# Expert weights prepared beside a dense block: steps queued behind the h copies, splits one step later, maxima in other banks

## The chip, the cores and the metric

The kernel runs on one core of a Trainium2 chip. The metric is the device time of one execution in microseconds (us); the time before is 1370.19 us, the median of 3 runs (1365.73 to 1371.75). The engines are PE (matmul), DVE (vector), ACT (scalar), POOL and SP, which issues most of the transfers.

## What is computed

Three layers follow one another. B = 8, H = 8, S = 576, D = 64; the 4608 tokens of 512 features that leave the first go through a dense layer of 2048 features and then through one of 8 experts of 1024 features each.

```python
kv = np.einsum('bhsd,bhse->bhde', k, v)
out = np.einsum('bhsd,bhde->bhse', q, kv)
rms = np.sqrt(np.mean(out * out, axis=-1, keepdims=True) + 1e-06)
x = (out / rms * g_norm).transpose(0, 2, 1, 3).reshape(B * S, H * D)
h = x @ w_in
g = np.maximum(h, 0.0) + alpha * np.minimum(h, 0.0)
x = g @ w_out
logits = x @ w_gate
e_idx = np.argmax(logits, axis=1)
...
for e in range(E):
    mask = e_idx == e
    h = np.maximum(x[mask] @ w1[e], 0.0)
    out[mask] = gate_w[mask, None] * eom[mask, e, None] * (h @ w2[e])
```

## The kernel before

Every large product is made in halves: each operand is split into a high and a low part in 16 bits, each scaled by a power of two taken from the operand's maximum, and three products (high by high, high by low, low by high) are summed.

The tokens are worked in 12 blocks of 384, three tiles of 128. Blocks 0 and 1 follow a plan written by hand, in which w_in and w_out are loaded and split (up to about 210 us). For each of the blocks 2 to 10 an h block is emitted and then a y block, and a scheduler that simulates the engines chooses the order on each engine within what the dependences and the buffers allow. Block 11's products stand in the order of the code. After it, from about 950 us, come the experts' own products, which read the prepared weights `ws` back from memory ("lanes").

An **h block** has 16 pieces. A piece is 12 products of 128x384 (line 688) into one of the two banks of `ps_h`; ACT copies the bank out as `m` (line 693), DVE bends it to `r` (line 702), ACT writes the high half of `g` (line 707) and DVE the low half (line 708). The pool `tp` holds two `m` and two `r`. The bank comes free with `m`. A **y block** has three tiles of 48 products of 128x512 (line 723) in the two banks of `ps_y`; ACT copies a tile out as `ysb` (line 735), and `y_tail` scales it to 16 bits (`row`, lines 775 and 779) and has SP transpose it (`yT`, line 788). The logits `l` (line 801) of a tile need yT and use the one bank of `ps_l`; DVE reads them out as `lg` (line 802), and `rk` (line 835) are counts for routing.

Beside these, `tick` hands out other work, one step at a time, after each piece of h and after every fifth f of a y tile. One kind is the **attention** of a later block: `kvps` (line 262, products of k and v), its maximum `allmaxkv` (lines 150 to 158), `kv` in 16 bits, then for each tile `ops` (line 349, products of kv with the transposed `qT`), `xs` (lines 358 and 399), `x` in halves (lines 410 and 415) and its transpose on SP (line 421), which is what the next h block multiplies. `x_3` is block 3's. qT is transposed on SP too (line 333).

The other kind is `expert_jobs`, the **expert weights**: 16 weight halves m (w1 and w2 of 8 experts), each in four parts of 128x1024. A step is either a magnitude (a raw load `rawe`, line 612, 512 KB, issued by SP; ACT takes absolute values, `eab`, line 623; DVE folds them into a running maximum `eam`, line 626) or a split (ACT `whi`, line 474; DVE `wlo`, line 475; two stores to `ws`, line 642, from ACT and SP). Between a weight's four magnitudes and its four splits stands its maximum: a transpose on PE (line 150, `allmax_w`), a reduction on DVE (`amrow`, line 152) and a product that spreads the result (line 154), in the bank `ps_l`. `tick(f % 3 == 0)` hands out an expert step after every third piece of h, `tick(1)` one after every fifth f of a y tile: 6 and 9 a block. Five raw parts fit in the pool `rawp`; the first magnitude of a weight issues the load of a part that is needed eight steps later in the list, and its first three splits each one that is needed five steps later.

Of the kernel before, what the change touches and what calls it, by code (L numbers as in the profile page):

```python
# [66 lines left out]
def body(ctx: ExitStack, tc, q, k, v, g_norm, w_in, w_out, alpha, w_gate, w_og, w1, w2, out):  # L67
# [79 lines left out]
    def all_max(am, nm):  # L147
        n = am.shape[1]
        ps = ps_l.tile([P, P + E], F32, tag="l", name="allmax" + nm)
# [327 lines left out]
    def finish_max(am, nm):  # L477
        m = small.tile([P, 1], F32, tag="amx", name="amx" + nm)
        dve.tensor_reduce(out=m, in_=am, axis=AX.X, op=ALU.max)
        return all_max(m, nm)  # L480
# [122 lines left out]
    def expert_jobs():  # L603
# [12 lines left out]
        for n in range(4):  # L616
            load(n)
        for m in range(2 * E):
            nm = f"_w{m}"
            am = cv.tile([P, 512], BF16, tag="acc", name="eam" + nm, bufs=1)  # L620
            for i in range(4):
                ab = cv.tile([P, 2, 512], BF16, tag="c", name=f"eab{nm}_{i}", bufs=3)
                act.activation(out=ab.rearrange("p a b -> p (a b)"), in_=raws[4 * m + i], func=AF.Abs)  # L623
                for h in range(2):
                    if i or h:
                        dve.tensor_tensor(out=am, in0=am if i else ab[:, 0, :], in1=ab[:, h, :], op=ALU.max)
                if i == 0:
                    load(4 * m + 4)
                yield
            for w in (256,):  # L630
                dve.tensor_tensor(out=am[:, 0:w], in0=am[:, 0:w], in1=am[:, w:2 * w], op=ALU.max)
            r = finish_max(am[:, 0:256], nm)
            s = small.tile([P, 1], F32, tag="es", name="es" + nm)
            inv = small.tile([P, 1], F32, tag=f"ei{m % 2}", name="ei" + nm)
            pow2(r, nm, s, inv)
            for i in range(4):
                w = ws[m // 2, :, m % 2 * 8192:(m % 2 + 1) * 8192].rearrange("p (t c) -> p t c", t=2)
                hi = stg.tile([P, 1024], F16, tag="hl", name=f"whi{nm}_{i}")
                lo = cv.tile([P, 1024], F16, tag="am", name=f"wlo{nm}_{i}")
                split(hi, lo, raws[4 * m + i], s)  # L640
                for t, (eng, x) in enumerate(((act, hi), (sp, lo))):
                    eng.dma_start(out=w[:, t, i * 1024:(i + 1) * 1024], in_=x)
                if i < 3:
                    load(4 * m + 5 + i)
                yield
            if m % 2 == 0:
                inv1 = inv
            else:
                dve.scalar_tensor_tensor(out=kexp[:, m // 2:m // 2 + 1], in0=inv1, scalar=1.0 / CB, in1=inv,
                                         op0=ALU.mult, op1=ALU.mult)  # L650


    attq, yq, exq, side = [], [], [], []

# [10 lines left out]
    def tick(n_expert=0):  # L665
        if yq:
            yq.pop(0)()
        if side:
            side.pop(0)()
        step(attq)  # L670
        for _ in range(n_expert):
            step(exq)
# [26 lines left out]
    def h_bend(f, part):  # L699
        i, r0 = part  # L700
        r = tp.tile([P, BLK], F32, tag="r", name=f"r_{i}_{f}")
        dve.scalar_tensor_tensor(out=r, in0=r0, scalar=alphat[:, f:f + 1], in1=r0, op0=ALU.mult, op1=ALU.max)  # L702
# [7 lines left out]
    def emit_h_block(i):  # L710
        for f in range(NF):
# [13 lines left out]
    def emit_y_block(i):  # L725
        b = y_state(i)
        for u in range(TB):
# [766 lines left out]
```

## Time and profile before

| what | value |
|---|---|
| runs, median (lowest, highest) | 1370.19 us (1365.73, 1371.75) |
| the profiled execution's own time | 1362.63 us |
| its span | 1360.9 us |
| PE busy | 1266.7 us, 93% |
| DVE busy | 827.1 us, 61% |
| ACT busy | 558.3 us, 41% |
| POOL busy | 333.1 us, 24% |
| bytes moved | 236.22 MB |

The profile follows one execution, and its time stands in the table beside the runs; the span is from its first to its last instruction. Busy shares are means over the whole span, so a stage has to be read from its own windows. A wait is the idle time of an engine just ahead of an instruction, put down to whatever released it last.

### The profile page before, as it was taken

How to read it: one execution, taken by the hardware profiler on the slowest of the kernel's cores; microseconds unless marked ns; L12 is line 12 of the kernel's file. 1: busy time of each engine (PE TensorE's matmuls, PEld its weight loads, DVE VectorE, ACT ScalarE, POOL GpSimd, SP SyncE). 2: the span in 40 equal slices, each digit the busy share in tenths (PEclk: the TensorE clock that was granted, in tenths of full speed). 3: DMA queues.
4: the chain of work that ended last, by engine and by line, in shares of the span. 5: the costliest groups of instructions: out<-in, count | busy, mean ns of one | idle time of the engine just before them, and what ended most of it. 6: DMA issues, size and time to landing. Idle time of an engine off the chain costs nothing. (4 is left out here: it accounts for less than half of the span.)

```text
span 1360.9 us, 21940 instructions
## 1 busy us (share of the span) xinstructions
PE 1266.7 (93%) x7681; PEld 660.8 (49%) x7681; DVE 827.1 (61%) x2316; ACT 558.3 (41%) x928; POOL 333.1 (24%) x410
## 2 busy tenths in 40 slices
PE   5588999949999998999999999999989999999998
PEld 4444455525555554555555555554434444444443
DVE  7999876768787887968687778562612221211221
ACT  3455663436454655655464656450111111111111
POOL 4312220332222232223132222102322222222211
PEclk9799999979999999999999999999989999999999
DMA  9653217647495956775736665306999799699852
GB/s 290 168 162 118 70 63 182 136 143 183 149 245 136 250 162 192 194 225 140 236 66 181 171 179 147 110 9 189 221 339 235 149 289 289 145 237 221 158 108 55
DMA packets 322497, 236.22 MB, mean 174 GB/s; under 512 B 245436, under 2 KB 278220, under 8 KB 317904
## 3 DMA queue, kind: packets, MB, share of 16 engines
q1 hardware_dynamic: 303760, 189.05, 55.5%
q0 software_dynamic: 9216, 28.94, 6.7%
q10 hardware_dynamic: 9408, 16.79, 3.7%
q8 instruction: 62, 1.02, 0.3%
q14 instruction: 51, 0.42, 0.1%
HBM read 248.34 MB, written 53.25 MB: 222 GB/s over the span
## 5 line engine op out<-in xcount | busy, mean ns | idle before, releaser
L723 PE MATMUL y<-wo,g 128*128 128x512 f16 x1728 | 401.2, 380 | 9.7 <-DVE xs L399 7.4
L688 PE MATMUL h<-x,wi 128*128 128x384 f16 x1920 | 340.3, 328 | 24.0 <-DMA x<-x 18.3
L688 PEld LDWEIGHTS <-wi 128*128 128x128 f16 x2304 | 221.7, 98 | 182.7 <-issue 35.7
L723 PEld LDWEIGHTS <-g 128*128 128x128 f16 x1728 | 164.8, 98 | 194.0 <-issue 9.9
L1200 DVE CAST h_d<-br_d 128x512 f16<-128x512 f32 x62 | 27.1, 438 | 259.8 <-ACT br_d L1198 132.7
L1216 PE MATMUL bo_d<-lane,hT_d 128*128 128x512 f16 x744 | 167.3, 382 | 7.5 <-DMA hT_d<-h_d 7.5
L1194 PE MATMUL bh_d<-lane,byT_d 128*128 128x512 f16 x744 | 165.3, 379 | 0.0
L707 ACT CAST g<-r 128x384 f16<-128x384 f32 x192 | 97.3, 509 | 131.4 <-DVE r L702 127.0
L702 DVE SCALAR_TENSOR_TENSOR r<-m,alphat 128x384 f32<-128x384 f32 x192 | 122.2, 639 | 20.5 <-ACT m L693 19.8
L1216 PEld LDWEIGHTS <-hT_d 128*128 128x128 f16 x744 | 72.8, 98 | 97.8 <-DMA hT_d<-h_d 9.0
L1194 PEld LDWEIGHTS <-byT_d 128*128 128x128 f16 x744 | 72.7, 98 | 88.1 <-issue 0.8
L375 POOL TENSOR_TENSOR rs<-ms,mhalf 128x8 f32<-128x8 f32 x36 | 66.4, 1848 | 185.5 <-DVE qm L381 138.0
L693 ACT ACTIVATE m<-h,scal 128x384 f32<-128x384 f32 x160 | 91.9, 575 | 36.0 <-PE h L688 34.0
L708 DVE TENSOR_TENSOR g<-r,g 128x384 f16<-128x384 f32 x160 | 91.7, 575 | 22.6 <-ACT g L707 21.6
L475 DVE SCALAR_TENSOR_TENSOR wlo_w<-rawe,es_w,whi_w 128x1024 f16<-128x1024 f32 x64 | 84.6, 1338 | 19.9 <-ACT whi_w L474 9.8
L867 POOL DMA_INDIRECT ytab<-row,pos x36 | 38.2, 1061 | 216.1 <-DVE pos L848 113.2
L1198 ACT ACTIVATE br_d<-bh_d 128x512 f32<-128x512 f32 x62 | 37.0, 597 | 131.0 <-PE bh_d L1194 109.2
L623 ACT ACTIVATE eab_w<-rawe 128x1024 bf16<-128x1024 f32 x64 | 67.1, 1055 | 47.3 <-DMA rawe<-in_moe_w_dram 45.3
L474 ACT ACTIVATE whi_w<-rawe,es_w 128x1024 f16<-128x1024 f32 x64 | 70.9, 1142 | 29.3 <-DVE es_w L144 15.7
L1220 POOL DMA_INDIRECT out_dram<-ob_d,oidx_d x31 | 31.4, 1013 | 206.2 <-ACT ob_d L1219 189.6
L1219 ACT ACTIVATE ob_d<-bo_d,msc_d 128x512 f32<-128x512 f32 x31 | 21.3, 687 | 139.9 <-PE bo_d L1216 139.9
L688 PE MATMUL hbank<-x,wi 128*128 128x384 f16 x384 | 67.0, 332 | 7.2 <-DMA x<-x 5.4
(365 smaller groups left out, 1367.9 us busy)
## 6 DMA issues: line engine op xcount, KB each, us to landing
lane<-ws SPq DMA_DIRECT2D x150, 1024.0 KB
rawe<-in_moe_w_dram SPq DMA_DIRECT2D x64, 512.0 KB
ws<-whi_w ACTq DMA_DIRECT2D x64, 256.0 KB
ws<-wlo_w SPq DMA_DIRECT2D x64, 256.0 KB
rawwi<-in_moe_w_in_dram SPq DMA_DIRECT2D x16, 512.0 KB
rawwo<-in_moe_w_out_dram SPq DMA_DIRECT2D x16, 512.0 KB
q<-in_q_dram SPq DMA_DIRECT2D x16, 512.0 KB
k<-in_k_dram SPq DMA_DIRECT2D x28, 256.0 KB
```

The costliest lines, as they stand in the source:

```text
L375: pool.tensor_tensor(out=rs, in0=ms, in1=mhalf, op=ALU.pow)
L474: act.activation(out=dst_h, in_=src, func=AF.Copy, scale=s)
L475: dve.scalar_tensor_tensor(out=dst_l, in0=src, scalar=s, in1=dst_h, op0=ALU.mult, op1=ALU.subtract)
L623: act.activation(out=ab.rearrange("p a b -> p (a b)"), in_=raws[4 * m + i], func=AF.Abs)
L688: pe.matmul(ps, wi[:, f // 4 * NC + c, w, fs], xt[i][:, xc, :], start=(n == 0), stop=(n == 3 * NC - 1))
L693: act.activation(out=r0, in_=ps, func=AF.Copy, scale=(scst if start else scal)[:, f:f + 1])
L702: dve.scalar_tensor_tensor(out=r, in0=r0, scalar=alphat[:, f:f + 1], in1=r0, op0=ALU.mult, op1=ALU.max)
L707: act.copy(out=hi, in_=r)
L708: (pool if start else dve).tensor_tensor(out=lo, in0=r, in1=hi, op=ALU.subtract)
L723: pe.matmul(ps, g[:, t, f % GF, us], wo[:, f, w, :], start=(start and m == 0), stop=(stop and m == 2), **kw)
L1194: pe.matmul(hp[ts], j["yT"][:, x, ts], w1_[:, w, c, hs], start=(m == 0), stop=(m == 3 * NC - 1))
L1216: pe.matmul(po[ts], hT[:, g, ts], w2_[:, w, f, :], start=(m == 0), stop=(m == 3 * NFE - 1))
```

## The change

Three things change. Each expert step's instructions on ACT and DVE are ordered behind the last h copy (or y copy) on ACT and the last bend on DVE that had been emitted when the step was handed out. The steps are listed in another order: magnitude 0 of the next weight stands ahead of the four splits of a weight, the maximum is taken in the step of the fourth magnitude, and each of the four splits issues one load, of the part that is five further on and needed four steps later; five parts are loaded at the start instead of four. And a weight's maximum takes its bank from `ps_y` while an h block is emitted and from `ps_h` while a y block is emitted, instead of from `ps_l`.

```diff
-    def all_max(am, nm):
+    def all_max(am, nm, pool_=None, tag="l"):
         n = am.shape[1]
-        ps = ps_l.tile([P, P + E], F32, tag="l", name="allmax" + nm)
+        ps = (pool_ or ps_l).tile([P, P + E], F32, tag=tag, name="allmax" + nm)
...
     def expert_jobs():
...
-        for n in range(4):
-            load(n)
-        for m in range(2 * E):
-            nm = f"_w{m}"
-            am = cv.tile([P, 512], BF16, tag="acc", name="eam" + nm, bufs=1)
-            for i in range(4):
-                ab = cv.tile([P, 2, 512], BF16, tag="c", name=f"eab{nm}_{i}", bufs=3)
-                act.activation(out=ab.rearrange("p a b -> p (a b)"), in_=raws[4 * m + i], func=AF.Abs)
-                for h in range(2):
-                    if i or h:
-                        dve.tensor_tensor(out=am, in0=am if i else ab[:, 0, :], in1=ab[:, h, :], op=ALU.max)
-                if i == 0:
-                    load(4 * m + 4)
-                yield
-            for w in (256,):
-                dve.tensor_tensor(out=am[:, 0:w], in0=am[:, 0:w], in1=am[:, w:2 * w], op=ALU.max)
-            r = finish_max(am[:, 0:256], nm)
...
+        def scale(m):
+            nm = f"_w{m}"
+            am = sums.pop(m)
+            dve.tensor_tensor(out=am[:, 0:256], in0=am[:, 0:256], in1=am[:, 256:512], op=ALU.max)
+            r = finish_max(am[:, 0:256], nm, *idle[0])
...
+        def halves(m, i):
+            nm = f"_w{m}"
+            w = ws[m // 2, :, m % 2 * 8192:(m % 2 + 1) * 8192].rearrange("p (t c) -> p t c", t=2)
+            hi = stg.tile([P, 1024], F16, tag="hl", name=f"whi{nm}_{i}")
+            lo = cv.tile([P, 1024], F16, tag="am", name=f"wlo{nm}_{i}")
+            split(hi, lo, raws[4 * m + i], scs[m][0])
+            for t, (eng, x) in enumerate(((act, hi), (sp, lo))):
+                eng.dma_start(out=w[:, t, i * 1024:(i + 1) * 1024], in_=x)
+            load(4 * m + 5 + i)
+
+        for n in range(5):
+            load(n)
+        magnitude(0, 0)
+        yield
+        for m in range(2 * E):
+            for i in range(1, 4):
+                magnitude(m, i)
+                if i == 3:
+                    scale(m)
+                yield
+            if m + 1 < 2 * E:
+                magnitude(m + 1, 0)
+                yield
             for i in range(4):
...
-                if i < 3:
-                    load(4 * m + 5 + i)
+                halves(m, i)
                 yield
...
+    paced, idle = {}, [None]
...
-        for _ in range(n_expert):
-            step(exq)
+        if n_expert and exq:
+            with ExitStack() as behind_h:
+                for ins in paced.values():
+                    behind_h.enter_context(tc.issue_after(ins))
+                step(exq)
...
-        act.activation(out=r0, in_=ps, func=AF.Copy, scale=(scst if start else scal)[:, f:f + 1])
+        t = act.activation(out=r0, in_=ps, func=AF.Copy, scale=(scst if start else scal)[:, f:f + 1])
+        paced["act"] = t.ins
...
+        paced["dve"] = t.ins
...
     def emit_h_block(i):
+        idle[0] = ps_y, "y"
...
     def emit_y_block(i):
         b = y_state(i)
+        idle[0] = ps_h, "h"
...
-                act.copy(out=ysb, in_=ps)
+                paced["act"] = act.copy(out=ysb, in_=ps).ins
```

Lines of the changed kernel are 21 to 25 higher from `h_sum` on (the h product is line 709, m 714, g 730, the y product 747, ysb 760, l 826), and eab is line 624.

On ACT, in block 5, the magnitudes of weight 6 stand like this before (`m_5_5` is the copy of piece 5 of block 5, `eab_w6_1` the magnitude of part 1 of weight 6, `g` the high half):

```order
L693 ACTIVATE m_5_5_5510<-h_5_5_5497,scal_145 128x384
L623 ACTIVATE eab_w6_1_5701<-rawe_25_5264 128x1024
L707 CAST g1_200<-r_5_4_5460 128x384
L693 ACTIVATE m_5_6_5539<-h_5_6_5526,scal_145 128x384
L707 CAST g1_200<-r_5_5_5512 128x384
L358 ACTIVATE xs_2_2_5477<-ops_2_2_5464 128x512
L623 ACTIVATE eab_w6_2_5797<-rawe_26_5342 128x1024
L288 CAST kv16_5_5396<-kvsc_5_5394 128x512
L707 CAST g1_200<-r_5_6_5541 128x384
L693 ACTIVATE m_5_7_5564<-h_5_7_5551,scal_145 128x384
L623 ACTIVATE eab_w6_3_5840<-rawe_27_5443 128x1024
```

and like this now:

```order
L714 ACTIVATE m_5_12_5676<-h_5_12_5663,scal_145 128x384
L624 ACTIVATE eab_w6_1_5701<-rawe_25_5339 128x1024
L730 CAST g3_202<-r_5_12_5678 128x384
L714 ACTIVATE m_5_13_5718<-h_5_13_5705,scal_145 128x384
L730 CAST g3_202<-r_5_13_5720 128x384
L714 ACTIVATE m_5_14_5737<-h_5_14_5724,scal_145 128x384
L730 CAST g3_202<-r_5_14_5739 128x384
L714 ACTIVATE m_5_15_5791<-h_5_15_5778,scal_145 128x384
L624 ACTIVATE eab_w6_2_5797<-rawe_26_5440 128x1024
L624 ACTIVATE eab_w6_3_5840<-rawe_27_5548 128x1024
L624 ACTIVATE eab_w7_0_5874<-rawe_28_5613 128x1024
```

The magnitude `eab_w6_1` stood behind piece 5 and two more were between pieces 6 and 8; now it stands behind piece 12, and the next three behind piece 15.

On PE, in block 3, y products of the same block (`y_3_0`, `y_3_1`) stand between the pieces of h before, runs of one name left out:

```order
L688 MATMUL h_3_5_3591<-x_3_2516,wi_203 128x384
...
L723 MATMUL y_3_0_3910<-wo_204,g0_199 128x512
...
L801 MATMUL l_2_0_3381<-wg16_147,yT_2_0_3171 128x32
...
L688 MATMUL h_3_6_3620<-x_3_2516,wi_203 128x384
...
L723 MATMUL y_3_1_4048<-wo_204,g0_199 128x512
...
L723 MATMUL y_3_0_3910<-wo_204,g1_200 128x512
...
L723 MATMUL y_3_1_4048<-wo_204,g1_200 128x512
...
L688 MATMUL h_3_7_3643<-x_3_2516,wi_203 128x384
```

and none do now, where only the logits of block 2 come between:

```order
L709 MATMUL h_3_4_3539<-x_3_2516,wi_203 128x384
...
L709 MATMUL h_3_5_3591<-x_3_2516,wi_203 128x384
...
L826 MATMUL l_2_2_3742<-wg16_147,yT_2_2_3412 128x32
...
L709 MATMUL h_3_6_3620<-x_3_2516,wi_203 128x384
...
L709 MATMUL h_3_7_3643<-x_3_2516,wi_203 128x384
```

The y products that stood between pieces 5 and 7 have moved behind the h block, as `y_3_0` now takes its bank after the maximum of a weight.

On PE, from the end of block 5 to the second product of attention in block 6, the first row of each name as it comes (the products of `ops_2_3`, `ops_2_4` and `ops_2_5` are those of three tiles of attention) is this before:

```order
L349 MATMUL ops_2_3_6001<-kv16_4_4440,qT_2_3_5836 128x128
...
L723 MATMUL y_5_1_5938<-wo_204,g3_202 128x512
...
L723 MATMUL y_5_2_6062<-wo_204,g0_199 128x512
...
L688 MATMUL h_6_0_6167<-x_6_5121,wi_203 128x384
...
L349 MATMUL ops_2_4_6186<-kv16_5_5396,qT_2_4_5910 128x128
...
L801 MATMUL l_5_0_6135<-wg16_147,yT_5_0_5936 128x32
...
L688 MATMUL h_6_1_6241<-x_6_5121,wi_203 128x384
...
L688 MATMUL h_6_2_6260<-x_6_5121,wi_203 128x384
...
L150 MATMUL allmax_w7_6222<-ident_62,amx_w7_6220 1x128
...
L349 MATMUL ops_2_5_6325<-kv16_5_5396,qT_2_5_6092 128x128
...
L688 MATMUL h_6_3_6279<-x_6_5121,wi_203 128x384
```

and this now:

```order
L349 MATMUL ops_2_3_5999<-kv16_4_4437,qT_2_3_5836 128x128
...
L747 MATMUL y_5_0_5803<-wo_204,g3_202 128x512
...
L150 MATMUL allmax_w6_5847<-ident_62,amx_w6_5845 1x128
...
L747 MATMUL y_5_1_5934<-wo_204,g3_202 128x512
...
L747 MATMUL y_5_2_6062<-wo_204,g0_199 128x512
...
L826 MATMUL l_5_0_6135<-wg16_147,yT_5_0_5932 128x32
...
L349 MATMUL ops_2_4_6201<-kv16_5_5393,qT_2_4_5906 128x128
...
L826 MATMUL l_5_1_6374<-wg16_147,yT_5_1_6060 128x32
...
L150 MATMUL allmax_w7_6152<-ident_62,amx_w7_6150 1x128
...
L709 MATMUL h_6_0_6182<-x_6_5121,wi_203 128x384
...
L349 MATMUL ops_2_5_6322<-kv16_5_5393,qT_2_5_6092 128x128
```

Between `ops_2_3` and `ops_2_5` there stood y_5_2 and three pieces of h, split by logits; now y_5_2, two sets of logits and one piece of h stand there, and the maxima of weights 6 and 7 are both taken in this stretch.

## Rows read from the trace of the kernel before

**Rows 1.** Page, part 1: busy us of each engine, share of the span, instructions.

```profile
PE 1266.7 (93%) x7681; PEld 660.8 (49%) x7681; DVE 827.1 (61%) x2316; ACT 558.3 (41%) x928; POOL 333.1 (24%) x410
```

**Rows 2.** Windows: busy us (instructions) of each engine, granted clock; two h stretches, a y stretch.

```profile
384.60:436.90 52.30, 49.22 (x356) 27.94 (x355) 45.68 (x135) 29.80 (x51) 12.66 (x9) 1.00 0.73 189
356.40:384.60 28.20, 25.67 (x154) 12.46 (x155) 19.50 (x46) 12.87 (x17) 6.78 (x9) 1.00 0.82 211
872.00:917.10 45.10, 45.10 (x284) 25.49 (x283) 25.82 (x77) 20.06 (x38) 3.23 (x8) 1.00 0.13 31
305.00:950.00 645.00, 625.38 (x4012) 338.81 (x4012) 483.83 (x1409) 340.75 (x553) 154.90 (x144) 0.99 0.61 167
```

**Rows 3.** Windows of line 723 alone, the y products, in h stretches 2 and 4.

```profile
210.70:261.70 51.00, 10.32 (x43) 4.31 (x44) 1.00 0.68 166
384.60:436.90 52.30, 13.31 (x52) 4.84 (x52) 1.00 0.73 189
```

**Rows 4.** Waits of PE, 305 to 950 us: us in total, times, longest.

```profile
PE h L688 <- ACT m L693: 5.6, 7, 2.0
PE ops L349 <- DMA qT<-q: 5.3, 4, 2.5
PE l L801 <- DMA yT<-row: 5.1, 4, 2.3
PE allmax_w L150 <- DVE lg L802: 2.3, 2, 1.4
PE y L723 <- DVE g L708: 0.9, 1, 0.9
```

**Rows 5.** Waits of PE, 210.7 to 305.1 us.

```profile
PE kvps L262 <- DMA v<-in_v_dram: 0.9, 2, 0.5
```

**Rows 6.** Line 623, the magnitudes on ACT: idle before them (us, times), one releaser.

```profile
  DMA rawe<-in_moe_w_dram: 45.3, 30
```

**Rows 7.** Timeline of ACT: start, us, operation, idle before it and its releaser.

```profile
417.62 1.06 ACT L623 ACTIVATE eab_w<-rawe 128x1024 bf16<-128x1024 f32 x1 [1.87 <-DMA rawe<-in_moe_w_dram]
```

**Rows 8.** Timeline of PE at four places.

```profile
242.62 0.23 PE L349 MATMUL ops<-kv,qT 128*128 128x128 f16 x1 [0.20 <-DMA qT<-q]
...
284.20 0.38 PE L158 MATMUL allmaxkv<-amdiagkv,ones 8*128 8x8 f32 x2
...
305.02 6.12 PE L688 MATMUL h<-x,wi 128*128 128x384 f16 x23 [17.36 <-DMA x<-x]
...
419.68 2.11 PE L688 MATMUL h<-x,wi 128*128 128x384 f16 x12 [2.01 <-ACT m L693]
...
520.68 0.83 PE L349 MATMUL ops<-kv,qT 128*128 128x128 f16 x12
521.36 11.20 PE L723 MATMUL y<-wo,g 128*128 128x512 f16 x51
...
543.39 0.73 PE L349 MATMUL ops<-kv,qT 128*128 128x128 f16 x10 [0.55 <-DMA qT<-q]
```

**Rows 9.** Timeline of SP's queue at two places.

```profile
300.47 2.00 SPq L421 DMA_TRANSPOSE x<-x  x1
...
540.18 1.26 SPq L333 DMA_TRANSPOSE qT<-q  x1
```

**Rows 10.** Lines of DVE, 305 to 950 us: busy us, mean ns, idle before.

```profile
L702 DVE SCALAR_TENSOR_TENSOR r<-m,alphat 128x384 f32<-128x384 f32 x144 | 90.8, 631 | 12.9 <-ACT m L693 12.6
L708 DVE TENSOR_TENSOR g<-r,g 128x384 f16<-128x384 f32 x144 | 82.9, 577 | 18.9 <-ACT g L707 18.1
...
L475 DVE SCALAR_TENSOR_TENSOR wlo_w<-rawe,es_w,whi_w 128x1024 f16<-128x1024 f32 x60 | 78.6, 1327 | 19.1 <-ACT whi_w L474 9.5 <-ACT row L775 3.7 <-DMA ws<-wlo_w 3.0
...
L626 DVE TENSOR_TENSOR eam_w<-eam_w,eab_w 128x512 bf16<-128x512 bf16 x86 | 36.8, 428 | 19.1 <-ACT eab_w L623 18.7
```

**Rows 11.** Windows at two waits of PE: PEclk is the granted clock.

```profile
420.00:422.00 2.00, 2.00 (x14) 1.17 (x12) 2.00 (x8) 1.13 (x3) 0.00 (x0) 1.00 0.22 68
767.00:770.00 3.00, 3.00 (x24) 1.99 (x25) 1.94 (x8) 0.45 (x1) 0.00 (x0) 0.50 1.01 249
```

More of the change, by code (lines that the diff above doesn't have):

```diff
@@ L475, in split, with finish_max @@
         dve.scalar_tensor_tensor(out=dst_l, in0=src, scalar=s, in1=dst_h, op0=ALU.mult, op1=ALU.subtract)
-    def finish_max(am, nm):
+    def finish_max(am, nm, *bank):
         m = small.tile([P, 1], F32, tag="amx", name="amx" + nm)
         dve.tensor_reduce(out=m, in_=am, axis=AX.X, op=ALU.max)
-        return all_max(m, nm)
+        return all_max(m, nm, *bank)
     class Dense:
@@ L614, in load, with magnitude @@
                 raws[n] = t
-        for n in range(4):
-            load(n)
-        for m in range(2 * E):
+        sums, scs = {}, {}
+        def magnitude(m, i):
             nm = f"_w{m}"
-            am = cv.tile([P, 512], BF16, tag="acc", name="eam" + nm, bufs=1)
-            for i in range(4):
-                ab = cv.tile([P, 2, 512], BF16, tag="c", name=f"eab{nm}_{i}", bufs=3)
-                act.activation(out=ab.rearrange("p a b -> p (a b)"), in_=raws[4 * m + i], func=AF.Abs)
-                for h in range(2):
-                    if i or h:
-                        dve.tensor_tensor(out=am, in0=am if i else ab[:, 0, :], in1=ab[:, h, :], op=ALU.max)
-                if i == 0:
-                    load(4 * m + 4)
-                yield
-            for w in (256,):
-                dve.tensor_tensor(out=am[:, 0:w], in0=am[:, 0:w], in1=am[:, w:2 * w], op=ALU.max)
-            r = finish_max(am[:, 0:256], nm)
+            if i == 0:
+                sums[m] = cv.tile([P, 512], BF16, tag="acc", name="eam" + nm, bufs=1)
+            am = sums[m]
+            ab = cv.tile([P, 2, 512], BF16, tag="c", name=f"eab{nm}_{i}", bufs=3)
+            act.activation(out=ab.rearrange("p a b -> p (a b)"), in_=raws[4 * m + i], func=AF.Abs)
+            for h in range(2):
+                if i or h:
+                    dve.tensor_tensor(out=am, in0=am if i else ab[:, 0, :], in1=ab[:, h, :], op=ALU.max)
+        def scale(m):
[3 more added lines that the diff above has]
+            r = finish_max(am[:, 0:256], nm, *idle[0])
             s = small.tile([P, 1], F32, tag="es", name="es" + nm)
@@ L635, in expert_jobs @@
             pow2(r, nm, s, inv)
-            for i in range(4):
[L637 to L642, printed above, removed]
-                if i < 3:
-                    load(4 * m + 5 + i)
-                yield
[L646 to L650, printed above, removed]
+            scs[m] = s, inv
+            if m % 2:
+                dve.scalar_tensor_tensor(out=kexp[:, m // 2:m // 2 + 1], in0=scs[m - 1][1], scalar=1.0 / CB, in1=inv,
+                                         op0=ALU.mult, op1=ALU.mult)
+        def halves(m, i):
[20 more added lines that the diff above has]
+                yield
+            for i in range(4):
+                halves(m, i)
+                yield
     attq, yq, exq, side = [], [], [], []
+    paced, idle = {}, [None]
     def step(gens):
@@ L701, in h_bend @@
         r = tp.tile([P, BLK], F32, tag="r", name=f"r_{i}_{f}")
-        dve.scalar_tensor_tensor(out=r, in0=r0, scalar=alphat[:, f:f + 1], in1=r0, op0=ALU.mult, op1=ALU.max)
+        t = dve.scalar_tensor_tensor(out=r, in0=r0, scalar=alphat[:, f:f + 1], in1=r0, op0=ALU.mult, op1=ALU.max)
+        paced["dve"] = t.ins
         return r
```

## Prediction

> **What bounds the kernel now.** I read the engines' busy time first: PE works 1266.7 us of the 1360.9 us span, DVE 827.1 [rows 1]. The change touches only the stretch in which expert weights are prepared beside the h and y blocks, 160 to 870 us. From 305 to 950 us PE is busy 625.4 of 645 us, so not 20 us of waits are there to be won, 17.4 of which are one wait at its start. Next I split that stretch: in the h stretch of block 4 PE has 49.2 of 52.3 us and DVE 45.7, in the y stretch ahead of it PE 25.7 of 28.2 and DVE 19.5 [rows 2]. DVE is nearly as full as PE in an h stretch and far from it in a y stretch. It doesn't bind there today because y products, 52 matmuls and 13.3 us of PE in block 4, 43 and 10.3 us in block 2, stand between the pieces of h [rows 3].
>
> Third, the waits of PE: for the copy m out of the h bank 5.6 us in 7 waits, for qT 5.3, for yT 5.1, for the shared bank of logits and maxima 2.3, for a low half of g 0.9 [rows 4]; ahead of that, in blocks 2 and 3's start, 0.9 for loads of v [rows 5]. Fourth, what makes m late: ACT sits 45.3 us in front of magnitudes whose raw weights have not landed [rows 6], and whatever is queued behind such a magnitude on ACT waits with it. At 417.62 one has waited 1.87 us for its load; the m behind it comes after it and xs, and PE waits 2.01 us, the longest of the seven [rows 7, 8].
>
> **The change part by part.** The sum is made against the profiled execution, 1362.63 us; it lies 7.6 us under the runs' median of 1370.19, and I carry the difference over unchanged.
>
> *Magnitudes behind the h copies, loads further ahead in steps.* Each m-to-magnitude pair is now ordered the other way: m first. Every part is now loaded four steps ahead of its magnitude, not five or eight, but a step can no longer be pulled forward to where its load has just been issued: four steps are twelve pieces of h (2.11 us each, [rows 8], 25 us) or sixty y products (13.31/52 = 0.26 us each, [rows 3], 15 us), against the 1.87 us by which that load was late. The wait that remains stands behind m, so what is late next is the bend's successor g and not PE's bank. I take 4 of the 5.6 us; bounds 0 (the seven have other causes) and -5.6. The 0.9 us for g have the same cause upstream (DVE's maxima come late and bunched): -1, bounds 0 and -1. **-5.0.**
>
> *Maxima in a bank of h or y.* A weight's transpose no longer waits for the reader of the logits: the 2.3 us go. **-2.3**, bounds 0 and -2.3. The price is the filler: while an h block is emitted its maximum takes the next turn of y's two banks, so y's first tile can't start until that maximum has been read. This is the term on which the sign hangs. The order shows blocks 3 and 4 without any y between pieces of h, blocks 2, 9 and 10 with none before piece 9 or 12.
>
> *What the lost filler costs.* In block 4, 52 y matmuls leave the h stretch, and with them the steps handed out after every 15th of them: 3.5 steps of the expert and of the attention. Per block DVE does 483.8/9 = 53.8 us between 305 and 950 (nine blocks, as 144 bends = 9 x 16 show) [rows 2]. Bends and low halves are (90.8+82.9)/9 = 19.3 of it, splits and maxima (78.6+36.8)/9 = 12.8, or 1.0 a step (115.4 us over some 117 steps); the rest, 21.7, is attention and routing, 0.9 for each of 25 hand-outs [rows 10]. 3.5 x 1.9 = 6.6 leave, so 39.1 of the 45.7 us stay in the h stretch. PE keeps 49.2-13.3 = 35.9. PE can be ahead of DVE by the two banks of h and the two copies m, four pieces, 8 us: 43.9. DVE busy all the time would fit; at the share that it has now, 45.7/52.3 = 0.87, it needs 45. So it is on the edge: I take **0**, since the waits on ACT that held DVE's share down are the ones that go. Bounds: 0, and 9.1 us a block (no slack at all) in blocks 3 and 4 with half of it in 2 and 9, together +27. Block 10 has cover whatever happens: DVE 25.8 of 45.1 us there [rows 2].
>
> *Waits that change place.* Products of qT and yT waited 10.4 us in eight waits [rows 4]. Without filler PE comes to some of them sooner. At block 6, ops_2_5 came 22.7 us after ops_2_3 (520.68 to 543.39) and still waited 0.55 for qT, which SP issued at 540.18 behind the transposed x of ops_2_3 [rows 8, 9]. Now 51 y (11.2 us), ops_2_4 (0.83), one piece of h (2.1) and 16 short logit products stand between: about 14.5 us. Unless ACT and DVE bring xs and x that much sooner, it waits up to 8 us. I take 3 there, as the q load and x are no longer behind four magnitudes and splits; and of the other seven waits I let half, 4.4 us, appear at other places. 3 + 4.4 - 10.4 = **-3.0**, bounds -9 and +8. In block 2 PE reaches the v products and ops_1_0 sooner by up to 10.3 us, the filler that went, and both waited already (0.9 us, and 0.20 at 242.62) [rows 5, 8]: **+3.5**, a third of it, since SP's loads are also a little earlier; bounds 0 and +10.
>
> *The wait for x_3.* The last product of its maximum stands at 284.20, its transpose is issued at 300.47, h_3_0 starts at 305.02 after 17.36 us of nothing [rows 8, 9]. In the new order the same number of y products follows the maximum (none), and two splits and the row's transpose still stand ahead on DVE and SP. **0**, bounds -5 and +5 (two splits, 1.3 us each [rows 10], and an ordering of two transposes).
>
> *Five magnitudes out of the first stage* and the re-ordered generator itself move 5 x 1.5 us of ACT and DVE from beside a full PE to beside a full PE: **0**. The last maximum ends in block 10 as before, so the stage with the experts' lanes starts no later.
>
> Sum: -5.0 -2.3 +0 -3.0 +3.5 +0 = **-6.8**: 1355.8 for a profile like the one of before, 1363 for the median.
>
> **A rule weighed against the trace.** After the 2.3 us wait for yT the granted clock of the next 3 us was 0.50, the lower of the two levels, 1.2 GHz; after the 2.01 us wait for m it was 1.00 [rows 4, 11]. Half clock for 3 us costs 1.5 us. The Trainium skill, "TensorE: Matmul & The Clock Gate", section "HAM oscillation — how this bites in real kernels", says that products in bursts with waits for DMA between them send the array back to half speed each time, so that each wait is paid again. The trace agrees for one of these two waits. By it alone every wait that my sum puts in new places would cost more, and it is the third rival.
>
> **Rivals.** (1) *The waits only change place* (0.15). For it: qT and yT waits are set by the chain ops, xs, x, SP, which the change doesn't shorten, and PE that no longer stops for m arrives sooner at the next of them. The -5.0 and -2.3 come back as 7 to 10 us there: 1370, from 1364 to 1378. Against it: ACT loses 45 us of standing in front of others' work.
>
> (2) *DVE becomes the bound of the h stretches* (0.20; slower). Place: bend and low half in blocks 3 and 4, and partly 2 and 9. It decides as soon as DVE with its gaps needs more than PE's 35.9 us plus the usable slack. With half the slack (4 us) and the share of now: 45 - 39.9 = 5.1 us in blocks 3 and 4, half of it in 2 and 9: +15, so 1363 + 15 = 1378; from 1370 to 1390. For it: 0.87 of the time was busy with filler there. Against it: the steps are now spread, one behind every third bend, and y stretches have 8 us of DVE to spare.
>
> (3) *Each new wait is paid twice by the clock* (0.07): some eight waits of 1 to 3 us without filler, at 1.5 us each, +12: 1375.
>
> (4) *More is won* (0.08): x_3 comes sooner because DVE is less bunched at the end of block 2 (-5) and the waits of rows 4 go without successors (-10.4 rather than -3): -20 at most, 1350.
>
> **How the numbers follow.** The likeliest case is the small gain (0.50), 1363, its own range 1354 to 1371. A measurement of this kernel can tell about 0.5% (7 us) from no change, so the case lies on that edge: 0.32 of it are faster, 0.18 the same. (4) gives 0.08 faster; (1) 0.11 same and 0.04 slower; (2) 0.04 and 0.16; (3) 0.04 and 0.03. Together faster 0.40, same 0.37, slower 0.23. The range of 1345 to 1383 takes in the three cases in the middle, most of the gain of (4) and the lower half of (2); about 0.15 is left out, most of it above.
>
> **What the profile will show.** Right: no magnitude with a load's wait of microseconds ahead of an m; PE's waits for m under 2 us in all and none for lg before a weight's transpose; h stretches of blocks 3 and 4 near 38 us, y stretches longer by 11 to 13; x_3 still late by 15 to 19 us. Wrong: waits of PE for m of 1 us and more at every piece of blocks 3 and 4, with DVE's bend behind splits (rival 2); waits for qT and yT over 10 us in sum (rival 1); many stretches at clock 0.50 (rival 3). What makes the forecast wrong most easily is the DVE share in blocks 3 and 4, then block 6's ops_2_5.

## The result, and the profile after

The changed kernel takes 1381.47 us (median of 4 runs, 1380.14 to 1385.33) against 1367.96 of the kernel before in the same comparison (its three runs and one more): ratio 1.0139, 95% interval 1.0103 to 1.0175. It is slower by 1.4%, where 1363 us were forecast. Its profiled execution took 1380.14 us, 17.5 more than that of before.

The engines do the same work; the first part of the page has the busy times:

```profile
PE 1273.4 (92%) x7681; PEld 662.7 (48%) x7681; DVE 828.2 (60%) x2316; ACT 559.1 (41%) x928; POOL 326.6 (24%) x410
```

PE is busy 6.7 us longer for the same 7681 products [rows 1], which already says that some of them ran at a lower clock. Next the two h stretches that were to decide the sign, those of blocks 3 and 4, and the y stretch behind block 4 (columns as in [rows 2]), then line 747 alone, the y products, in the two h stretches:

```profile
313.20:353.40 40.20, 38.88 (x292) 23.83 (x293) 34.72 (x103) 25.73 (x46) 13.31 (x11) 0.96 0.60 153
387.60:425.90 38.30, 38.30 (x314) 22.99 (x312) 35.41 (x105) 24.70 (x44) 8.72 (x6) 1.00 0.73 198
...
425.90:467.10 41.20, 36.59 (x191) 17.06 (x191) 23.57 (x70) 16.73 (x22) 9.35 (x11) 0.92 0.60 180
```

```profile
313.20:353.40 40.20, 0.02 (x1) 0.11 (x2) 0.96 0.60 153
387.60:425.90 38.30, 0.14 (x1) 0.00 (x0) 1.00 0.73 198
```

The filler (the y products between the pieces of h) is gone, as the order of the instructions said, and that costs nothing there: in block 4 PE is busy for all of the 38.30 us and DVE for 35.41. What is lost stands behind this stretch: 4.6 us of PE's 41.20 us in the y stretch are idle, and the clock there is 0.92. The waits of PE say where, from 300 to 965 us:

```profile
PE l L826 <- DMA yT<-row: 24.6, 5, 16.3
PE allmax_w L150 <- DVE amx_w L479: 4.6, 1, 4.6
PE h L709 <- ACT m L714: 3.5, 5, 1.7
PE l L826 <- DVE st L371: 2.9, 1, 2.9
PE allmax_w L150 <- DVE xinv L388: 2.1, 1, 2.1
PE ops L349 <- DMA qT<-q: 1.8, 2, 1.3
```

Against [rows 4], the waits for m and qT are 5.3 us together instead of 10.9, and the one for lg is gone. In their place the wait for yT is longer, and there are waits that were not there, for a weight's maximum and behind statistics of the attention. They are few and long. On PE, at the end of block 2 and of blocks 4 and 5:

```profile
281.21 0.37 PE L826 MATMUL l<-wg,yT 128*128 128x32 f16 x8 [5.69 <-DMA rawe<-in_moe_w_dram]
281.43 6.79 PE L747 MATMUL y<-wo,g 128*128 128x512 f16 x21
...
294.09 0.38 PE L158 MATMUL allmaxkv<-amdiagkv,ones 8*128 8x8 f32 x2
...
311.73 0.40 PE L826 MATMUL l<-wg,yT 128*128 128x32 f16 x8 [16.29 <-DMA yT<-row]
313.16 5.66 PE L709 MATMUL h<-x,wi 128*128 128x384 f16 x24 [1.03 <-DMA x<-x]
...
430.51 0.37 PE L150 MATMUL allmax_w<-ident,amx_w 128*1 128x128 f32 x1 [4.61 <-DVE amx_w L479]
...
538.39 0.39 PE L826 MATMUL l<-wg,yT 128*128 128x32 f16 x8 [4.25 <-DMA yT<-row]
...
543.67 0.39 PE L826 MATMUL l<-wg,yT 128*128 128x32 f16 x8 [2.94 <-DVE st L371]
546.16 0.37 PE L150 MATMUL allmax_w<-ident,amx_w 128*1 128x128 f32 x1 [2.09 <-DVE xinv L388]
```

The 16.29 us hide the wait for x_3, which would have lasted to 313.16 in any case: the maximum of kv that x_3 needs is at 294.09 instead of 284.20 [rows 8], and h_3_0 starts 19 us behind it, where it was 21. So the question in block 2 is what made the maximum late. The first two rows are most of it: 5.69 us of waiting, and 21 y products behind it in 6.79 us at a lower clock, which costs 2.2 us by the account below, together 7.9 of 9.9 us. Before, the y products at this place ran at full clock:

```profile
274.51 4.48 PE L723 MATMUL y<-wo,g 128*128 128x512 f16 x20
```

For the wait the profile names a raw load; DVE's rows show the chain:

```profile
269.97 2.47 DVE L475 SCALAR_TENSOR_TENSOR wlo_w<-rawe,es_w,whi_w 128x1024 f16<-128x1024 f32 x2
...
274.71 1.28 DVE L475 SCALAR_TENSOR_TENSOR wlo_w<-rawe,es_w,whi_w 128x1024 f16<-128x1024 f32 x1 [1.70 <-DMA ws<-wlo_w]
279.78 1.28 DVE L475 SCALAR_TENSOR_TENSOR wlo_w<-rawe,es_w,whi_w 128x1024 f16<-128x1024 f32 x1 [3.78 <-DMA ws<-wlo_w]
280.98 0.18 DVE L827 TENSOR_REDUCE lg<-l 128x16 f32<-128x32 f32 x1
```

The logits at 281.21 need the one bank of logits, its reader `lg` runs at 280.98, and ahead of it on DVE stand four splits, two of which waited for the store of an earlier split to free its buffer.

Behind each of the long waits the clock is at the lower of its two levels (three stretches of 2 us, PEclk is the third number from the right):

```profile
282.00:284.00 2.00, 2.00 (x7) 0.66 (x5) 1.99 (x11) 0.99 (x2) 0.00 (x0) 0.50 0.99 312
...
432.00:434.00 2.00, 2.00 (x6) 0.72 (x5) 0.00 (x0) 0.00 (x0) 1.17 (x2) 0.50 0.23 93
548.00:550.00 2.00, 2.00 (x8) 0.84 (x6) 0.38 (x1) 0.62 (x1) 0.76 (x1) 0.50 0.00 0
```

**The account.** From the first h product of block 2 to the last y product of block 11 I split the time of a kernel into three: the idle time ahead of PE's instructions, PE's busy time in windows of 2 us times what the granted clock lacked of 1 (the price of the clock), and the rest. Before: 737.6 us = 39.9 idle + 3.7 clock + 694.0. After: 757.7 = 51.7 + 12.3 + 693.7. The difference of 20.1 us is 11.8 of waits and 8.6 of clock, less 0.3 in the rest; 10.3 of it lie in block 2 and 9.8 behind it. (The stage ahead of block 2 is 2.2 us and the one behind block 11 0.4 us shorter, hence 17.5 for the whole.) In all 20 profiled executions of this study the rest is 691 to 696 us: no edit changed PE's work, so waits and clock are all that there is to explain.

### The profile page after: what moved, and what is told of

It reads as the page before. It is cut to its first block, busy times and chain, and to the rows that moved or that the text cites. A ratio compares the mean times of both kernels' runs of the same rounds, so it can differ in the third digit from the quotient of the medians.

```text
span 1378.4 us, 21922 instructions
## 1 busy us (share of the span) xinstructions
PE 1273.4 (92%) x7681; PEld 662.7 (48%) x7681; DVE 828.2 (60%) x2316; ACT 559.1 (41%) x928; POOL 326.6 (24%) x410
## 5 line engine op out<-in xcount | busy, mean ns | idle before, releaser
L747 PE MATMUL y<-wo,g 128*128 128x512 f16 x1728 | 396.6, 384 | 9.9 <-DVE xs L399 7.4
L724 DVE SCALAR_TENSOR_TENSOR r<-m,alphat 128x384 f32<-128x384 f32 x192 | 125.0, 653 | 28.9 <-ACT m L714 27.0
L731 DVE TENSOR_TENSOR g<-r,g 128x384 f16<-128x384 f32 x160 | 90.4, 566 | 18.1 <-ACT g L730 17.5
L892 POOL DMA_INDIRECT ytab<-row,pos x36 | 41.0, 1138 | 202.5 <-DVE pos L873 71.5
L624 ACT ACTIVATE eab_w<-rawe 128x1024 bf16<-128x1024 f32 x64 | 66.3, 1050 | 31.6 <-DMA rawe<-in_moe_w_dram 28.8
```

The costliest lines, as they stand in the source:

```text
L724: t = dve.scalar_tensor_tensor(out=r, in0=r0, scalar=alphat[:, f:f + 1], in1=r0, op0=ALU.mult, op1=ALU.max)
L731: (pool if start else dve).tensor_tensor(out=lo, in0=r, in1=hi, op=ALU.subtract)
L747: pe.matmul(ps, g[:, t, f % GF, us], wo[:, f, w, :], start=(start and m == 0), stop=(stop and m == 2), **kw)
```

## The experiments

Three parts of the change can be had singly: the queueing (P), the new order of steps and loads (O), the bank (B). The edits, each against the kernel that has the part:

```diff
# without P
-        if n_expert and exq:
-            with ExitStack() as behind_h:
-                for ins in paced.values():
-                    behind_h.enter_context(tc.issue_after(ins))
-                step(exq)
+        for _ in range(n_expert):
+            step(exq)
# without B
-            r = finish_max(am[:, 0:256], nm, *idle[0])
+            r = finish_max(am[:, 0:256], nm)
# without O: expert_jobs() of the kernel before
```

P and O:

> Steps queued behind the copies and in the new order, but the weights' maxima in the old bank of logits. Theory A (the bank is the cause: y's first tile stands behind a maximum, so the h blocks have no filler and PE meets long waits at the ends of blocks): the y products are back between the pieces of h, waits of PE over 2.5 us after 205 us fall from six to the one for x_3, reduced clock costs 4 us instead of 12, and the time is that of before or below, 1358 to 1370 us, ratio 0.990 to 1.002. Theory B (the new order of the steps, with loads only four steps ahead, makes raw weights late and the logits' reader stand behind splits): still 1376 to 1385, ratio 1.007 to 1.013. Theory C (the queueing behind copies): the same as B here.

P and B:

> Steps queued behind the copies and the maxima in banks of h or y, but the old order of the steps and loads. Theory A (bank): still slow, 1376 to 1390 us, ratio 1.007 to 1.016. Theory B (order): 1362 to 1371, ratio 0.996 to 1.003. Theory C (queueing): slow as well, ratio 1.007 or more.

O and B:

> New order of the steps and the maxima in banks of h or y, but the steps not queued behind the copies. Theory A (bank) and theory B (order): slow, ratio 1.007 to 1.016. Theory C (queueing behind copies is the cause): 1360 to 1371, ratio 0.995 to 1.003.

B alone:

> Only the maxima are moved to banks of h or y; order and queueing as before. Theory A (bank): the h blocks lose their y filler and the time rises to 1376 to 1390 us, ratio 1.007 to 1.016. Theories B and C: no change, 0.996 to 1.004.

P alone:

> Only the queueing of steps behind the copies; order of steps, loads and bank as before. Theory D (the queueing and the new order each push magnitudes and splits into the stretch at a block's end where x and yT are made, so PE meets waits there, and both add up): 1.004 to 1.009, five magnitudes gone from the first stage, two or more waits of PE over 2.5 us besides the one for x_3. Theory E (only the combination hurts): 0.997 to 1.003.

O alone:

> Only the new order of the steps and loads; no queueing, old bank. Theory D (each adds): 1.003 to 1.008, with x_3's product later than 305 us by 5 or more. Theory E (only the combination hurts): 0.997 to 1.003.

Measured, with the two stretches of the profiled execution (block 2: from its first h product to that of block 3; blocks 3 to 11: from there to the last y product), the idle time of PE and the price of the clock in both together, and the splits and magnitudes that ran within block 2:

| kernel | ratio (95%) | block 2, us | blocks 3-11, us | idle, us | clock, us | splits / magnitudes in block 2 |
|---|---|---|---|---|---|---|
| before | 1 | 94.3 | 643.3 | 39.9 | 3.7 | 4 / 2 |
| P | 0.9949 (0.9914-0.9983) | 97.2 | 636.8 | 35.4 | 6.5 | 4 / 7 |
| O | 1.0035 (1.0005-1.0065) | 100.7 | 640.5 | 42.8 | 2.9 | 6 / 4 |
| B | 0.9976 (0.9943-1.0009) | 90.6 | 649.0 | 34.0 | 12.6 | 4 / 4 |
| P, O | 1.0077 (1.0042-1.0111) | 102.6 | 646.7 | 48.6 | 9.2 | 6 / 9 |
| P, B | 1.0059 (1.0022-1.0097) | 94.6 | 647.5 | 39.9 | 8.7 | 4 / 8 |
| O, B | 1.0034 (0.9992-1.0076) | 101.7 | 637.2 | 42.3 | 3.7 | 8 / 7 |
| P, O, B | 1.0139 (1.0103-1.0175) | 104.6 | 653.1 | 51.7 | 12.3 | 6 / 9 |

The stretches, the idle time and the clock are those of one execution of each kernel, which lay between 7.5 us under and 5.0 us over the median of its kernel's runs over all kernels of this study (P with B: 6.8 under), so differences of a few us between them can be chance.

Theory A, that the bank does the harm, falls: the bank alone changes nothing that stands out of the noise. The other theories don't hold whole either: P with B and O with B lie between what was expected, and P alone lies below what D and E expected. No single part is the cause, and the parts don't add: P alone makes the kernel faster, P with either of the others slower than either by itself (for P and O against O alone the intervals overlap). Two readings stand out. With O, block 2 takes 100.7 to 104.6 us, without it 90.6 to 97.2. And blocks 3 to 11 are longest with all three. The price of the clock doesn't follow the idle time: B alone has 12.6 us of it at 34.0 us idle, O alone 2.9 at 42.8.

The next two take the changed kernel apart in other ways, the transfers and the engine on which the queueing acts:

```diff
# without raw loads after the first five
-            if n < 8 * E:
+            if 5 <= n < 8 * E:
+                raws[n] = raws[n % 5]
+            elif n < 8 * E:
                 m, i = divmod(n, 4)
# queued on ACT alone
-                for ins in paced.values():
+                for ins in [paced["act"]]:
```

> The changed kernel with the raw weights' loads after the first five left out: the later parts are read from the five that are there, so 59 transfers of 512 KB are missing and the prepared weights are of the wrong parts; all else is issued. Theory F (raw loads that land late hold ACT in front of magnitudes, and ysb, x and yT behind them): the waits of PE for yT and logits at the ends of blocks 4, 5 and 7 go, 1355 to 1366 us, ratio 0.993 to 1.002. Theory D (it is where the steps stand on DVE and ACT, whatever the loads do): 1373 or more, ratio 1.007 to 1.014.

> The changed kernel with steps queued behind ACT's copies alone, not behind DVE's bends. If the queueing hurts through DVE (maxima and splits pushed behind bends into the end of a block): 1.003 to 1.008, as with order and bank alone. If it hurts through ACT (magnitudes and high halves behind the copies): 1.011 to 1.016, as the changed kernel.

Without the loads the changed kernel has ratio 1.0035 (1.0009 to 1.0061), 99.0 and 642.8 us: between the two theories and nearer to F's. Of the waits at the ends of blocks 5 and 7 for yT and a statistic (4.25, 2.94 and 2.90 us) one of 1.90 us is left, and one of 3.09 us came in block 9. But the wait for a weight's maximum at the end of block 4 stays:

```profile
424.97 0.37 PE L150 MATMUL allmax_w<-ident,amx_w 128*1 128x128 f32 x1 [4.88 <-DVE amx_w L479]
```

So it is not made by loads. ACT of the changed kernel shows how it comes about there:

```profile
426.67 0.57 ACT L714 ACTIVATE m<-h,scal 128x384 f32<-128x384 f32 x1
427.15 1.99 ACT L624 ACTIVATE eab_w<-rawe 128x1024 bf16<-128x1024 f32 x2
```

The last copy of the h block comes first, and two magnitudes that are queued behind it follow. The first of them is the weight's fourth, which its maximum at 430.51 needs, and y's first tile takes its bank behind the maximum, so PE has nothing to do until then. The maximum at the end of block 5 also still waits, 2.08 us instead of 2.09.

Queued on ACT alone the changed kernel has 1.0104 (1.0027 to 1.0182), just under what was expected for harm by ACT, and 100.2 and 650.9 us. Its trace has waits of 4.63, 4.42, 2.98 and 2.75 us at the same places. This points to ACT's part, though the interval reaches down to where DVE's part would matter too.

The loads needed a control, and block 2 a direct test. Empty steps ahead of the first weight's splits hand these, and every expert step behind them, out later and change nothing else in the code:

```diff
+            if m == 0:
+                for _ in range(10):
+                    yield
             for i in range(4):
                 halves(m, i)
```

> The changed kernel with ten empty steps ahead of the first weight's splits, so that its four splits, with their loads and stores, stand behind block 3's first bend instead of ahead of the maximum of kv that x_3 waits for. Theory G (these four splits on DVE and their stores are what makes block 2 ten us longer): from the first product of block 2 to that of block 3 falls from 104.6 to 91 to 96 us, and the ratio from 1.014 to 1.003 to 1.008, the rest being the waits at the ends of blocks 4, 5 and 7. Theory H (block 2 is longer for want of y filler or by the magnitudes that left the first stage): 101 us or more, ratio 1.010 or more.

> Queueing and new order with the old bank, and the same ten empty steps. Theory G: block 2 takes 90 to 96 us instead of 102.6, ratio from 1.008 to 0.995 to 1.002. Theory H: as without the empty steps, 100 us or more and 1.006 or more.

> Only the queueing, with ten empty steps ahead of the first weight's splits: three splits that stood between the maximum of kv and x_3's transpose go behind block 3's start. Theory G: x_3 comes 3 to 5 us sooner, 92 to 95 us for block 2 instead of 97.2, ratio 0.988 to 0.994 against 0.995 without. Theory H: no change, 0.993 to 0.998.

> The kernel before with the raw weights' loads after the first five left out, as in the changed kernel without them, and so with wrong weights prepared. Without these loads the changed kernel fell from 1.014 to 1.0035. If late loads hurt the changed kernel above all (theory F): this one gains little, ratio 0.996 to 1.002. If loads cost both kernels the same: 0.986 to 0.993.

With ten empty steps block 2 takes 92.6 us instead of 104.6 with all three parts, 94.7 instead of 102.6 with P and O, 93.0 instead of 97.2 with P alone. The place is right. On PE, of the kernel with all three:

```profile
284.94 0.38 PE L158 MATMUL allmaxkv<-amdiagkv,ones 8*128 8x8 f32 x2
...
299.73 0.40 PE L829 MATMUL l<-wg,yT 128*128 128x32 f16 x8 [13.30 <-DMA yT<-row]
301.69 1.76 PE L712 MATMUL h<-x,wi 128*128 128x384 f16 x5 [1.57 <-DMA x<-x]
```

The maximum of kv is at 284.94 instead of 294.09, and the ratio is 1.0073 (1.0046 to 1.0100), half of the loss gone, as theory G had it. But with P and O the ratio went only from 1.0077 to 1.0069 (1.0042 to 1.0096), though its profiled block 2 was 7.9 us shorter (that execution, 1366.23 us, was the fastest of six, with a median of 1370.22), and with P alone it rose to 1.0060 (1.0023 to 1.0097), since blocks 3 to 11 took 654.1 us instead of 636.8. Both are misses. The kernel before without raw loads has 0.9933 (0.9901 to 0.9964): the loads cost it 0.7%, the changed kernel 1.0%, which the intervals don't tell apart. The loads are a tax on both.

That empty steps can lengthen blocks that lie behind them asked for a control with fewer:

> The changed kernel with four empty steps instead of ten: by the order of its instructions all four splits of the first weight still stand ahead of the maximum of kv. A control for the empty steps themselves. Theory G (the place of the four splits decides block 2): block 2 takes 99 to 106 us, ratio 1.008 to 1.016. If ten empty steps helped only by shifting everything: 97 us or less.

> The kernel before with four empty steps ahead of the first weight's splits and nothing else. Theory K (from block 3 on the sum of waits and of half clock depends on which order the scheduler happens to find, so any edit moves it by some 5 to 10 us either way): from the first product of block 3 to the last y product of block 11 it differs from 643 us by 4 us or more, ratio off 1 by 0.003 to 0.008 on either side. Theory L (that stretch follows from queueing, order and bank): 640 to 646 us, ratio 0.996 to 1.002.

> Only the queueing, with four empty steps. The queueing alone gave 0.995 and 636.8 us from block 3 on, with ten empty steps 1.006 and 654.1. Theory K: anywhere from 634 to 656 us, off both by 3 us or more. Theory L: within 3 us of 636.8 and 0.992 to 0.997, with ten steps as the odd one.

| kernel | ratio (95%) | block 2, us | blocks 3-11, us | idle, us | clock, us | splits / magnitudes in block 2 |
|---|---|---|---|---|---|---|
| P, O, B + 4 | 1.0059 (1.0031-1.0087) | 93.8 | 652.0 | 46.2 | 7.3 | 4 / 7 |
| P, O, B + 10 | 1.0073 (1.0046-1.0100) | 92.6 | 655.7 | 43.3 | 13.1 | 0 / 5 |
| before + 4 | 0.9990 (0.9955-1.0025) | 95.1 | 640.5 | 37.7 | 3.8 | 4 / 3 |
| P + 4 | 0.9935 (0.9908-0.9962) | 98.8 | 631.0 | 33.9 | 4.9 | 4 / 7 |
| P + 10 | 1.0060 (1.0023-1.0097) | 93.0 | 654.1 | 44.8 | 8.1 | 1 / 4 |

Theory G falls in the form that I gave it. With four empty steps all four splits still stand ahead of the maximum of kv, and block 2 is as short as with ten. Their place alone doesn't do the harm. What differs is that less weight work is crowded into block 2, six splits and nine magnitudes with the change, four and seven here, and that the idle time ahead of splits on DVE in block 2 is 1.7 us instead of 5.5. The changed kernel without raw loads, with six and nine as well, tells these two apart; DVE's third and fourth split and PE's logits in block 2:

```profile
274.78 2.55 DVE L475 SCALAR_TENSOR_TENSOR wlo_w<-rawe,es_w,whi_w 128x1024 f16<-128x1024 f32 x2 [1.20 <-DMA ws<-wlo_w]
```

```profile
277.48 0.35 PE L828 MATMUL l<-wg,yT 128*128 128x32 f16 x8 [1.38 <-DVE lg L829]
```

With the same splits ahead of `lg`, but 1.20 us of waiting for stores instead of 5.5, PE waits 1.38 us instead of 5.69, the maximum of kv is at 287.92 instead of 294.09, and block 2 takes 99.0 us. So in the changed kernel some 6 of the 9.9 us by which the maximum is late go with the splits' wait for their stores, beside the raw loads. The splits behind the maximum count too: from its last product to block 3's first it took 16.3 to 17.4 us where at most one split ran between the two, 18.8 to 20.8 with two, and 20.7 to 25.1 with three to five. Over all 20 executions block 2 takes 90.6 to 98.8 us (mean 94.5) where up to four splits ran in it, and 97.9 to 104.6 (mean 101.2) where five to eight did; but the numbers alone don't decide, as four splits and seven magnitudes stand beside 93.8, 97.2 and 98.8 us. Four empty steps change the kernel before by nothing, so theory K, that any edit moves blocks 3 to 11 by 5 to 10 us, falls too for that kernel; with the queueing, 631.0, 636.8 and 654.1 us stand side by side, 631.0 outside what either theory expected, and why ten steps hurt there I don't know.

The last three ask why P wins alone and loses in company. In the second, the h blocks' maxima are back in the bank of logits (`idle[0] = ps_l, "l"` in `emit_h_block`):

> The changed kernel once more, unaltered, so that it stands beside the two others on one chip: 1.010 to 1.016, 104 us for block 2 and 651 to 656 us from block 3 on, as every kernel with all three parts had.

> The changed kernel with ten empty steps, with the maxima of h blocks back in the bank of logits (those of y blocks stay in a bank of h). Theory M (with the queueing a weight's maximum comes at an h block's last piece, and y's first tile stands behind it in the rotation of the banks): the waits of 3.8 to 4.7 us of PE for a maximum go, and from block 3 on it takes 645 to 649 us instead of 655.7, ratio 1.000 to 1.005. If the bank isn't the reason: 652 us or more, 1.005 or more.

> Queueing and new order, old bank, and the raw loads after the first five left out, so that wrong weights are prepared. With the loads it took 646.7 us from block 3 on, the queueing alone 636.8 and 631.0. The kernel before won 14 us there without these loads, the changed one 10. If the queueing and the new order hurt each other by the shorter lead of the loads: 16 us or more won, 631 us or less. If by something else: 8 to 14 us won, 633 to 639.

The unaltered kernel has 1.0113 (1.0057 to 1.0169), 103.2 and 650.7 us, with waits of 4.63, 4.24 and 2.92 us at the same three places as above: these places belong to the kernel and not to one execution. Its wait at the logits in block 2, 4.96 us, the profile itself puts down to `lg`. Theory M is wrong. With the h blocks' maxima in the old bank the kernel is the slowest of all, 1.0195 (1.0142 to 1.0247), 664.0 us from block 3 on. PE at the start of block 4:

```profile
395.07 0.37 PE L150 MATMUL allmax_w<-ident,amx_w 128*1 128x128 f32 x1 [7.20 <-DVE amx_w L479]
395.24 1.16 PE L712 MATMUL h<-x,wi 128*128 128x384 f16 x3
```

Here it is a y block's maximum, in a bank of h, that stands ahead of the next h piece and waits 7.2 us for its last magnitude. The wait doesn't belong to one bank: wherever a late maximum takes its turn ahead of a product, the product waits for it. Over the 20 traces this sorts the kernels: from block 3 on, PE waits 6.7 to 14.7 us in sum for weights' maxima in all seven that have queueing, new order and other banks together, whole or in part, with or without raw loads, and 0.0 to 2.8 us in the thirteen others. So waits of this size belong to no part and no pair, but to the three together.

Of theory F's question the third gives the other half. P and O without raw loads take 626.2 us from block 3 on, 20.5 less than with them, where the kernel before won 14.4 (643.3 to 628.9) and the changed one 10.3 (653.1 to 642.8). The ratio is 0.9908 (0.9874 to 0.9942), a fall of 1.7% against 0.7%. The profiled executions lay 2.0 us under their median with P and O, 6.6 and 7.2 us with the kernel before and the changed one, so the ratios are the surer measure. Beside the changed kernel without loads (1.0035) this also gives the price of the bank beside P and O where no load disturbs: 1.3%, or 642.8 against 626.2 us.

On ACT, with P and O magnitudes waited for raw loads 44.9 us (first row), with P alone 35.5 (second), in the changed kernel 28.8 (third):

```profile
  DMA rawe<-in_moe_w_dram: 44.9, 22
```

```profile
  DMA rawe<-in_moe_w_dram: 35.5, 19
```

```profile
  DMA rawe<-in_moe_w_dram: 28.8, 19
```

Before, it was 45.3 us [rows 6], so this sum doesn't sort the kernels: that the loads carry the loss of P and O is shown, that they do so by landing late is not.

## Why the prediction was wrong, step by step

**What bounds the kernel.** One reading was wrong: the 17.4 us wait for x_3 ends at 305.02, so it isn't part of the 20 us that PE is idle from 305 to 950; these are the other waits of [rows 4], 19.2 us in sum.

**The magnitudes, and the waits for m (-5.0).** The mechanism holds, the size was less: waits for m went from 5.6 to 3.5 us, -2.1 and not under the 2 us in all that I had named, and ACT's wait for raw loads from 45.3 to 28.8 us [rows 4, 6]; PE still waits once for a half of g (0.8 us against 0.9). The loads are fewer steps ahead than they were, four and not five or eight, whatever the step's title says. With P alone the rows are those that I described:

```profile
PE h L692 <- DMA x<-x: 19.7, 1, 19.7
PE l L809 <- DMA yT<-row: 5.6, 3, 3.9
PE ops L349 <- DMA qT<-q: 4.3, 5, 2.9
PE h L692 <- ACT m L697: 1.7, 4, 0.7
```

Waits for m are 1.7 us, and the kernel is faster by 0.5%.

**The bank (-2.3).** The wait of a maximum behind lg is gone. But the sum knew only the reader ahead of the maximum; it had no term for what the maximum makes wait. 4.6 and 2.1 us of waits for the maximum's own input came instead, so that a loss of 4.4 us, without the clock, stands where 2.3 were to be won. This step failed too.

**The lost filler (0).** Right, and rival 2 with it wrong: the h stretches of blocks 3 and 4 have 40.2 and 38.3 us, near the 38 that the part on what the profile will show had, and DVE keeps up. The forecast's worst fear didn't come; that the time rose as rival 2 had it (1370 to 1390) is no point for it.

**Waits that change place (-3.0 and +3.5).** Half of the seven other waits is 4.9 and not 4.4, so the first term should have been -2.5. The products of qT won: 5.3 to 1.8 us; ops_2_5 no longer waits microseconds. The logits lost: without the 16.3 us that hide x_3's wait, yT costs 24.6 - 16.3 = 8.3 us against 5.1, and 2.9 more came that the profile puts down to a statistic on DVE. These are the waits of rival 1, but not in exchange for others: idle time from block 3 on rose from 19.6 to 24.6 us. In block 2 the waits for v and qT went from 1.1 to 2.7 us, +1.6 where +3.5 was taken.

**Five magnitudes and the re-ordered generator (0).** This step failed most: 10.3 of the 20.1 us. I put it at nothing because PE is full in both places. What I didn't count is DVE, ACT and the transfers of block 2, at whose end stands the longest wait of the kernel, x_3's. The new order takes the first maximum a step earlier, so six splits instead of four ran in block 2, with six loads instead of three, beside nine magnitudes instead of two, four of the splits ahead of the logits' reader and two of these held up by stores, and block 2 grew by 10.3 us. My bound of 5 for x_3 looked at the chain behind the maximum of kv, which took 19 us against 21; what moved was its start.

**The clock (no term).** Rival 3, at 0.07, came on top of the other steps: 8.6 of the 20.1 us. The rule that I quoted stands in the Trainium skill, "TensorE: Matmul & The Clock Gate", section "HAM oscillation — how this bites in real kernels". The trace agrees, with 0.50 behind the waits of 5.69 and 4.61 us, though both were waits for DVE, and those from 538 to 546 us. The longest of the seven waits for m of before, 2.01 us, cost no clock [rows 11], nor did one of 2.53 us for qT at 382.09:

```profile
382.50:385.50 3.00, 3.00 (x38) 1.97 (x36) 2.48 (x5) 0.80 (x2) 0.78 (x1) 1.00 1.12 295
```

So exchanging many short waits for a few long ones can lose even at an equal sum. Length isn't all of it: 2.27 us cost clock before [rows 11], and with B alone two waits of 1.63 and 1.59 us, at 259.77 and 263.31, were followed by 0.50.

What the runs show is thus: O lengthens block 2 (by 5.4 to 11.1 us, each kernel with it against the same without; undone by empty steps), and from block 3 on the changed kernel loses 9.8 us in few long waits and in clock. Of these waits, those for a weight's maximum come at this size only where all three parts meet, and they stay when the raw loads go. That the raw loads carry the loss of P and O together is shown by leaving them out. What B costs beside P and O depends on the rest: nothing that stands out with ten empty steps, 1.3% without raw loads. Where the loss of P and B together comes from stays open, and without a prediction of the scheduler's order the loss of P with ten empty steps isn't explained either. The queueing alone (0.9949), and with four empty steps (0.9935, 0.9908 to 0.9962), beats both kernels.

## What to carry to other kernels

Split the bound engine's time into work, idle and clock first: here the work was the same within 0.7% in twenty executions, and the price of the clock could not be had from the sum of the waits. When steps are moved, count them in the stretch that holds the longest wait, on every engine and queue, and not only where the bound engine is full. And test the parts of a change singly and in pairs: here the part that wins by itself is the one that loses in company.

## What the runs showed of the hardware that was not expected

The clock fell to 0.50 in stretches behind waits of 2.1 to 5.7 us at four places of the changed kernel besides x_3's. Of its price, 12.3 us in all, 10.5 us lie behind these four places, about half of the 22.5 us of waits there (5.69; 4.61; 4.25, 2.94 and 2.09; and 2.90 at 626 us). Leaving out 59 loads of 512 KB, none of which PE reads, made the kernel before faster by 0.7% and the one with P and O by 1.7%.
